# Batch 0 loaded in order of need, last products of batch 0 on VectorE and ACT, projections of quad 1 ahead of the sums of quad 0, scaled values as separate steps

## The chip, the cores and the metric

The kernel runs on one core of a Trainium2 chip. The metric is the device time in microseconds of one execution, the median of several runs. The kernel uses five engines, each with its own instruction queue that is worked through in order: TensorE (PE) for matrix products and transposes, VectorE (DVE), ScalarE (ACT) for exponentials and copies, GpSimd (POOL) for arithmetic on SBUF and for issuing transfers that change the type, and SyncE (SP), which issues transfers. Sixteen transfer engines serve the queues of GpSimd and SyncE. Matrix products land in PSUM; everything else lies in SBUF.

## The reference

Eight batches of eight heads, 576 positions, head size 64, 128 features. Linear attention with exponential features, then one layer of an expert with an ELU:

```
proj = x @ w_phi                                  # x is q or k, per head: 576x64 @ 64x128
phi(x) = [exp(proj - m), exp(-(proj - m))]        # m = max |proj| of the row
kv  = phi(k)^T @ v ;  z = sum over positions of phi(k)
att = (phi(q) @ kv) / (phi(q) . z + 1e-6)
x   = att, heads side by side: 4608 x 512
h   = x @ w_in                                    # 512 x 2048
g   = h if h > 0 else exp(min(h, 0)) - 1
out = g @ w_out                                   # 2048 x 512, fp32
```

## The kernel before

The eight heads of a batch are worked in two quads of four heads; there are 16 quads. Quad i is batch i // 2. Of the 576 positions of a head 512 are the main rows, four to a partition, and 64 are the tail rows, which two heads share in one tile.

A quad has these steps, each a list of small functions in the dictionary that `attention_steps` returns. `tr`: eight transposes and one for the tails on TensorE for k, then for q, each followed by copies out of PSUM (L134, L137). `k`: five projections (four heads and the tails, L153), each with a maximum of |proj| on VectorE (L161) and two exponentials on ACT (EK, L174). The maximum isn't subtracted; instead `scale` takes em = exp(-m) and exp(m) on ACT (L182) and multiplies v by it on GpSimd: a cast (L187), four products of 128x512 (L192) and two of 128x128 (L200); these scaled values are vs. `q`: five projections of q for their maxima alone. `qf`: q's features with positions along the columns (L209, L217), and w = exp(2m). `kv`: the sums phi(k)^T v over positions, two groups of 20 products (L250, L262) with a copy to SBUF by ACT. `out`: four heads and the tails of phi(q) kv (L283, L308), the two signs put together on VectorE (L293, L299), then the division: a reciprocal on VectorE and two products of 128x576 on GpSimd that give x (L331). `x`: nine transposes of x (L341, L353) and two copies into xT.

The expert works on chunks of 512 rows, one for each batch and a ninth for all the tails. A unit of the first product (`mm1`, 16 for a chunk): four matmuls into ph (L386), an exponential on ACT (e_sb, L394), e - 1 on GpSimd (u_sb, L396), and max(ph, min(u, 0)) on VectorE (gT, L399). A unit of the second (`mm2`, four for a chunk): 16 matmuls into po (L407), a copy by ACT, a transfer out. Units are called between the attention's steps when they are due by a steady count of units per slot.

The program goes through slots: slot n does the projections and features of quad n (`new`), the sums of quad n - 1 (`old`), and the transposes of quad n + 1 (`nxt`), in an order that `slot_steps` writes out. Slot 0 has no old quad; slot 2 is the first at whose end the expert has work. The calls are not yet the order of the instructions: a planner orders them for each engine by its own forecast of when each is ready, with the earlier call first among those that are ready, and then sets the semaphores.

Loads: k and q are changed from fp32 to bf16 by the transfer and are issued by GpSimd; v stays fp32 and is issued by SyncE. Batch 0 is loaded in halves (heads 0 to 3 with the tails, then heads 4 to 7). `extra` is a list of further GpSimd transfers (eight of w_in, four calls for k and q of batch 1, eight of w_out), one taken after each step in slots 0 and 1 and after each third step later. `load_v(1)` is called after the scale step of quad 0. Tiles for k, q and v have two buffers, so batch b + 2 is loaded when batch b is done with them; the sums `tot` have one buffer.

## Time and profile before

| | |
|---|---|
| median of 3 runs | 472.37 us (471.5 to 473.35) |
| profiled execution | 472.63 us, span 470.9 us |
| TensorE busy | 406.8 us (86%) |
| VectorE busy | 279.0 us (59%) |
| ACT busy | 262.6 us (56%) |
| GpSimd busy | 247.7 us (53%) |
| chain that ended last | TensorE 51%, GpSimd 20%, ACT 11%, VectorE 8%, issue 5%, transfers 4% |

The span is the time from the first to the last instruction of the profiled execution; its own time has 1.7 us around it. Matmuls are pipelined and their ends are modelled, so a busy TensorE need not run at its peak.

### The profile page before, as it was taken

Reading aid. Unit: us, or ns where it says so; the run is one execution under the profiler, and the core shown is the slowest. Engines: PE = TensorE matmul, PEld = TensorE weight load, DVE = VectorE, ACT = ScalarE, POOL = GpSimd, SP = SyncE. Lnnn points to the kernel's source line nnn. Section 1 sums busy time; section 2 is a strip of 40 time slices with the busy share of each in tenths; the row PEclk is TensorE's granted clock in tenths of the full one; section 3 lists DMA queues with packets and bytes.
Section 4 is the critical chain, followed back from the end, with each engine's and each line's share of the span. In section 5 each row is a group of like instructions: output and inputs, shape, how many; then the busy total and the mean of one; then the engine's idle time right before and its main releaser. Section 6 shows DMA issues by size and latency. Waiting matters only on the chain.

```text
span 470.9 us, 8519 instructions
## 1 busy us (share of the span) xinstructions
PE 406.8 (86%) x3248; PEld 224.3 (48%) x3248; DVE 279.0 (59%) x596; ACT 262.6 (56%) x581; POOL 247.7 (53%) x360
## 2 busy tenths in 40 slices
PE   1674687899989998999898979799869898999995
PEld 0352444455546454646463636365536454444442
DVE  1564465974598359937992577738766755434420
ACT  1563074772888287746764548456738572543431
POOL 6388636836673568445943473716372643423420
PEclk9977787999999999999998999999989999999999
DMA  9999905331723181219201931010000000110113
GB/s 176 230 138 200 223 1 61 42 120 51 107 28 98 58 121 34 74 67 125 94 9 45 141 79 30 1 68 24 2 0 24 22 24 24 45 46 23 46 45 67
DMA packets 46329, 33.12 MB, mean 70 GB/s; under 512 B 14416, under 2 KB 41168, under 8 KB 46288
## 3 DMA queue, kind: packets, MB, share of 16 engines
q0 software_dynamic: 28192, 13.64, 22.6%
q1 hardware_dynamic: 18096, 18.94, 12.8%
q8 instruction: 25, 0.41, 0.4%
q14 instruction: 16, 0.13, 0.1%
HBM read 36.77 MB, written 9.44 MB: 98 GB/s over the span
## 4 chain that ended last, share of the span: by engine, by line
PE 51%; POOL 20%; ACT 11%; DVE 8%; issue 5%; DMA 4%; POOLq 0%; ACTq 0%
PE po L407 23%; PE ph L386 13%; POOL vs L192 7%; ACT EK L174 5%; POOL u_sb L396 4%; DMA q_b<-in_q_dram 4%; POOL x L331 3%; PE pkv L250 3%; DVE gT L399 3%; PE pk L153 3%; ACT e_sb L394 3%; ACT Eq L217 2%; PE tr L133 2%; POOL vs L200 2%; PE tr L341 2%
## 5 line engine op out<-in xcount | busy, mean ns | idle before, releaser
L396 POOL TENSOR_SCALAR u_sb<-e_sb 128x512 bf16<-128x512 f32 x144 | 87.3, 617 | 129.9 <-ACT e_sb L394 120.9
L386 PE MATMUL ph<-xT,w_in_sb 128*128 128x512 bf16 x512 | 139.9, 386 | 12.0 <-DVE gT L399 11.6
L407 PE MATMUL po<-w_out_sb,gT 128*128 128x512 bf16 x576 | 139.7, 383 | 4.2 <-DVE gT L399 4.2
L399 DVE SCALAR_TENSOR_TENSOR gT<-u_sb,ph 128x512 bf16<-128x512 bf16 x144 | 96.6, 681 | 68.5 <-POOL u_sb L396 67.7
L394 ACT ACTIVATE e_sb<-ph 128x512 f32<-128x512 f32 x144 | 86.0, 633 | 47.5 <-PE ph L386 47.3
L407 PEld LDWEIGHTS <-gT 128*128 128x128 bf16 x576 | 54.7, 99 | 63.1 <-DVE gT L399 5.1
L174 ACT ACTIVATE EK<-pk 128x512 bf16<-128x512 f32 x128 | 67.9, 624 | 26.7 <-DVE m_k L161 26.3
L386 PEld LDWEIGHTS <-w_in_sb 128*128 128x128 bf16 x576 | 52.2, 98 | 58.5 <-issue 20.3
L217 ACT ACTIVATE Eq<-pq 128x512 bf16<-128x512 f32 x128 | 65.9, 638 | 18.4 <-PE pq L209 18.3
L192 POOL TENSOR_TENSOR vs<-v_b,em 128x512 bf16<-128x512 f32 x64 | 65.3, 1043 | 17.5 <-ACT em L182 17.4
L415 ACT COPY o_sb<-po 128x512 f32<-128x512 f32 x36 | 21.5, 596 | 82.4 <-PE po L407 76.3
L161 DVE TENSOR_REDUCE m_k<-pk 128x4 f32<-128x512 f32 (+1 forms) x80 | 49.0, 632 | 19.3 <-PE pk L153 19.0
L161 DVE TENSOR_REDUCE m_q<-pk 128x4 f32<-128x512 f32 (+1 forms) x80 | 49.0, 624 | 9.0 <-PE pk L153 8.7
L331 POOL TENSOR_TENSOR x<-tot,rec 128x576 bf16<-128x576 f32 x32 | 36.0, 1146 | 15.7 <-DVE rec L328 15.6
L283 PEld LDWEIGHTS <-Eq 128*128 128x128 bf16 x512 | 29.2, 99 | 22.7 <-issue 9.1
L283 PE MATMUL pn<-kv,Eq 128*128 128x65 bf16 x512 | 33.5, 195 | 2.9 <-ACT EK L174 1.9
L293 DVE TENSOR_TENSOR tot<-pn,w 128x260 f32<-128x260 f32 x64 | 27.0, 422 | 10.4 <-PE pn L283 10.2
L134 DVE COPY kT<-tr 128x1024 bf16<-128x1024 bf16 x16 | 11.0, 690 | 36.6 <-PE tr L133 36.6
L153 PE MATMUL pk<-w_phi_both,qT 128*128 128x256 bf16 x144 | 28.3, 290 | 3.0 <-ACT EK L174 1.8
L153 PE MATMUL pk<-w_phi_both,kT 128*128 128x256 bf16 x144 | 28.9, 295 | 1.8 <-ACT EK L174 0.9
L209 PE MATMUL pq<-qT,w_phi_both 128*128 128x512 bf16 x64 | 22.8, 421 | 4.9 <-DVE m_q L161 2.8
L299 DVE TENSOR_TENSOR tot<-tot,pn 128x260 f32<-128x260 f32 x64 | 26.6, 417 | 0.4
(56 smaller groups left out, 363.5 us busy)
## 6 DMA issues: line engine op xcount, KB each, us to landing
out_dram<-o_sb SPq DMA_DIRECT2D x32, 256.0 KB, 2.3
v_b<-in_v_dram SPq DMA_DIRECT2D x7, 1024.0 KB, 5.7
k_b<-in_k_dram POOLq DMA_DIRECT2D x7, 512.0 KB, 7.8
q_b<-in_q_dram POOLq DMA_DIRECT2D x7, 512.0 KB, 8.2
w_in_sb<-in_moe_w_in_dram POOLq DMA_DIRECT2D x8, 256.0 KB, 12.4
w_out_sb<-in_moe_w_out_dram POOLq DMA_DIRECT2D x8, 256.0 KB, 8.5
v_b<-in_v_dram SPq DMA_DIRECT2D x2, 512.0 KB, 7.2
v_b<-in_v_dram SPq DMA_DIRECT2D x16, 64.0 KB, 5.4
```

Of the source, the lines that this page charges most:

```text
L153: nc.tensor.matmul(pk[:, 2 * j:2 * j + 2, :].rearrange("p a b -> p (a b)"), xT[:, 2 * hh + j, :], w_phi_rhs, start=True, stop=True,)
L161: nc.vector.tensor_reduce(m[:, o:o + NT] if hh < 4 else m[:, NS - 1::NS], pk[:, 0:2 * n, :], axis=AX.X, op=ALU.max, apply_absolute_value=True,
L174: nc.scalar.activation(dst, pk, ACT.Exp, scale=1.0 - 2.0 * sg)
L192: nc.gpsimd.tensor_tensor(vs[:, sg, r, 0:D], vb[:, o:o + 2 * HW].rearrange("p (n d) -> p n d", d=D), em[:, sg, r, None].to_broadcast((P, 2 ...
L217: nc.scalar.activation(st["Eq"][:, par, c, sg, :], pq, ACT.Exp, scale=1.0 - 2.0 * sg)
L283: nc.tensor.matmul(pt[:, t, :], st["Eq"][:, par, c, sg, o:o + P], st["kv"][:, s, c, sg, :], start=True, stop=True,)
L331: nc.gpsimd.tensor_tensor(st["x"][:, :, c, :], st["tot"][:, r, 0:D], rec[:, r, None].to_broadcast((P, NS, D)), op=ALU.mult,)
L386: nc.tensor.matmul(ph, w_in_sb[:, ct, jt * P:(jt + 1) * P], xTs[ch][:, ct, :], start=(ct == 0), stop=(ct == N_CT - 1),)
L394: nc.scalar.activation(e_sb, ph, ACT.Exp)
L396: nc.gpsimd.tensor_scalar(u_sb, e_sb, -1.0, 1.0, op0=ALU.add, op1=ALU.mult)
L399: nc.vector.scalar_tensor_tensor(gTs[ch][:, jt, :], u_sb, 0.0, ph, op0=ALU.min, op1=ALU.max)
L407: nc.tensor.matmul(po, gT[:, jt, tt * P:(tt + 1) * P], w_out_sb[:, jt, :], start=(jt == 0), stop=(jt == N_JT - 1),)
```

## The change

- Transfers of batch 0: v's first half with its tails and v's second half are issued by GpSimd, behind k and q of the same half, instead of by SyncE. Three of the w_in transfers are called before slot 0; the rest of `extra` is taken after steps 17 and later of slot 0, after each step of slot 1 and each third step later.
- `load_v(1)` is called after the scale step of quad 1. Instead of a memset, VectorE copies a column of em of quad 1 into the first column of v's main and tail parts, so that the load depends on em.
- The copies of q's transposes are on ACT instead of VectorE for both quads of batch 0.
- The scaled values and the two products of the division are on VectorE instead of GpSimd for quad 1.
- `k_scale` keeps em and the cast; the six products become steps `vs` of their own, `v_scaled`, with new places in each slot.
- Slot 0: the transposes of quad 1 come after the second q projection. Slot 1: the k projections and em of quad 1 come first, then kv of quad 0, then q projections of quad 1, sums of quad 0 and vs of quad 1 in turn. x_out of quad 0 moves from the end of slot 1 to behind kv of quad 1 in slot 2.

The whole diff, without its unchanged surroundings where they say nothing:

```diff
@@ -118,9 +118,11 @@
             )
 
 
+    states = {}
+
     def attention_steps(i):
         b, qd = divmod(i, 2)
-        st = {}
+        st = states[i] = {}
 
         def transposes(n):
             src = kqv[b][n]
@@ -131,10 +133,11 @@
             for j in range(8):
                 o = m0 + j * P
                 nc.tensor.transpose(tr[:, j, :], src[:, o:o + P], ident)
-            nc.vector.tensor_copy(dst[:, 0:8, :], tr)
+            copy = nc.scalar.copy if n == 1 and b == 0 else nc.vector.tensor_copy
+            copy(dst[:, 0:8, :], tr)
             trt = apsum.tile([P, P], BF16, name="trt", tag="ap")
             nc.tensor.transpose(trt, src[:, t0:t0 + P], ident)
-            nc.vector.tensor_copy(dst[:, 8, :], trt)
+            copy(dst[:, 8, :], trt)
             if n == 0:
                 st["m_k"] = small.tile([P, 2 * NS], FP32, name="m_k")
                 st["EK"] = work.tile([P, 4, 2, NT * F], BF16, name="EK")
@@ -176,33 +179,32 @@
         def q_head(hh):
             project(st["qT"], hh, st["m_q"])
 
+
+        eng = nc.vector if i == 1 else nc.gpsimd
+
         def k_scale():
-            em = small.tile([P, 2, 2 * NS], FP32, name="em")
+            em = st["em"] = small.tile([P, 2, 2 * NS], FP32, name="em")
             for sg in range(2):
                 nc.scalar.activation(
                     em[:, sg, :], st["m_k"], ACT.Exp, scale=2.0 * sg - 1.0
                 )
-            vb = kqv[b][2]
             vs = st["vs"] = work.tile([P, 2, 2 * NS, D1], BF16, name="vs")
-            nc.gpsimd.tensor_copy(vs[:, :, :, D], em)
-            for c in range(2):
-                for sg in range(2):
-                    r = slice(c * NS, c * NS + 2 * NT)
-                    o = (4 * qd + 2 * c) * HW
-                    nc.gpsimd.tensor_tensor(
-                        vs[:, sg, r, 0:D],
-                        vb[:, o:o + 2 * HW].rearrange("p (n d) -> p n d", d=D),
-                        em[:, sg, r, None].to_broadcast((P, 2 * NT, D)),
-                        op=ALU.mult,
-                    )
-            t0 = BW + qd * P
-            for sg in range(2):
-                nc.gpsimd.tensor_tensor(
-                    vs[:, sg, NS - 1::NS, 0:D],
-                    vb[:, t0:t0 + P].rearrange("p (n d) -> p n d", d=D),
-                    em[:, sg, NS - 1::NS, None].to_broadcast((P, 2, D)),
-                    op=ALU.mult,
-                )
+            eng.tensor_copy(vs[:, :, :, D], em)
+
+        def v_scaled(sg, c):
+
+            if c < 2:
+                r = slice(c * NS, c * NS + 2 * NT)
+                o, n = (4 * qd + 2 * c) * HW, 2 * NT
+            else:
+                r = slice(NS - 1, None, NS)
+                o, n = BW + qd * P, 2
+            eng.tensor_tensor(
+                st["vs"][:, sg, r, 0:D],
+                kqv[b][2][:, o:o + n * D].rearrange("p (n d) -> p n d", d=D),
+                st["em"][:, sg, r, None].to_broadcast((P, n, D)),
+                op=ALU.mult,
+            )
 
         def q_features(par, c):
             pq = apsum.tile([P, 4 * P], FP32, name="pq", tag="ap")
@@ -328,7 +330,7 @@
             nc.vector.reciprocal(rec, den)
             for c in range(2):
                 r = slice(c * NS, (c + 1) * NS)
-                nc.gpsimd.tensor_tensor(
+                eng.tensor_tensor(
                     st["x"][:, :, c, :],
                     st["tot"][:, r, 0:D],
                     rec[:, r, None].to_broadcast((P, NS, D)),
@@ -366,6 +368,7 @@
             "tr": [each(transposes, n) for n in range(2)],
             "k": [each(k_head, hh) for hh in range(5)],
             "scale": [k_scale],
+            "vs": [each(v_scaled, sg, c) for c in range(3) for sg in range(2)],
             "q": [each(q_head, hh) for hh in range(5)],
             "qf": [each(q_features, par, c) for c in range(2) for par in range(2)]
             + [q_features_tail],
@@ -451,24 +454,38 @@
 
     def slot_steps(n):
         old, new, nxt = quads.get(n - 1), quads.get(n), quads.get(n + 1)
-        if not old:
-            return new["k"] + new["scale"] + new["q"] + new["qf"] + nxt["tr"]
+        if n == 0:
+            return (
+                new["k"] + new["scale"] + new["q"][:2] + nxt["tr"] + new["q"][2:]
+                + new["vs"] + new["qf"]
+            )
+        if n == 1:
+            steps = new["k"] + new["scale"] + old["kv"]
+            for j in range(5):
+                steps += new["q"][j:j + 1] + old["out"][j:j + 1]
+                steps += new["vs"][j:j + 1]
+            return steps + new["vs"][5:] + new["qf"] + nxt["tr"]
         if n == 2:
 
             return (
-                old["kv"] + old["out"] + old["x"]
+                old["kv"] + quads[0]["x"] + old["out"] + old["x"]
                 + [lambda: chunk_ready(0)]
-                + new["k"] + new["scale"] + new["q"] + new["qf"] + nxt["tr"]
-            )
-        none = {"k": [], "q": [], "scale": [], "qf": []}
-        kk, qq = (new or none)["k"], (new or none)["q"]
+                + new["k"] + new["scale"] + new["q"] + new["vs"] + new["qf"]
+                + nxt["tr"]
+            )
+        none = {"k": [], "q": [], "scale": [], "qf": [], "vs": []}
+        new = new or none
+        kk, qq, vv = new["k"], new["q"], new["vs"]
         steps = (
             old["kv"][:1] + kk[:1] + old["kv"][1:] + kk[1:3]
             + old["out"][:1] + kk[3:4] + old["out"][1:2] + kk[4:]
-            + (new or none)["scale"]
-            + old["out"][2:3] + qq[:1] + old["out"][3:4] + qq[1:2]
-            + old["out"][4:] + qq[2:] + (new or none)["qf"]
-        )
+            + new["scale"]
+            + old["out"][2:3] + vv[:1] + qq[:1] + old["out"][3:4] + vv[1:2]
+            + qq[1:2] + old["out"][4:] + vv[2:3]
+            + qq[2:4] + vv[3:4] + qq[4:]
+        )
+        for j in range(5):
+            steps += new["qf"][j:j + 1] + vv[4 + j:5 + j]
         if nxt:
             steps += nxt["tr"]
         steps += old["x"]
@@ -482,18 +499,15 @@
     wst = consts.tile([P, F], FP32)
     for c in range(2):
         nc.sync.dma_start(out=wst[c * D:(c + 1) * D, :], in_=w_phi)
-    for n in range(2):
+    for n in range(3):
         load_main(nc.gpsimd, n, 0, 0, 4)
         load_tails(nc.gpsimd, n, 0)
-    load_main(nc.sync, 2, 0, 0, 4)
-    load_tails(nc.sync, 2, 0)
     nc.vector.memset(w_phi_both, 0.0)
     for c in range(2):
         r = slice(c * D, (c + 1) * D)
         nc.vector.tensor_copy(w_phi_both[r, c, :], wst[r, :])
-    for n in range(2):
+    for n in range(3):
         load_main(nc.gpsimd, n, 0, 4, 8)
-    load_main(nc.sync, 2, 0, 4, 8)
 
     quads[0] = attention_steps(0)
     for step in quads[0]["tr"]:
@@ -509,17 +523,21 @@
             )
         ]
 
-    def load_v(b, gate=False):
-        if gate:
-            nc.vector.memset(kqv[b][2][:, 0:1], 0.0)
+    def load_v(b, after=None):
+        if after is not None:
+
+            for o in (0, BW):
+                nc.vector.tensor_copy(kqv[b][2][:, o:o + 1], after)
         load_main(nc.sync, 2, b, 0, 8)
         load_tails(nc.sync, 2, b)
 
-    extra = [
+    w_in_loads = [
         lambda ct=ct, c=c: load_w_in(ct, c) for ct in range(N_CT) for c in range(2)
     ]
-    extra += load_kq(1)
-    extra += [lambda jt=jt: load_w_out(jt) for jt in range(0, N_JT, 2)]
+    w_out_loads = [lambda jt=jt: load_w_out(jt) for jt in range(0, N_JT, 2)]
+    for f in w_in_loads[:3]:
+        f()
+    extra = w_in_loads[3:] + load_kq(1) + w_out_loads
 
     UNITS = 136
     done = 0
@@ -533,9 +551,9 @@
         steps = slot_steps(n)
         for j, step in enumerate(steps):
             step()
-            if n == 0 and step is quads[0]["scale"][0]:
-                load_v(1, gate=True)
-            if extra and (n < 2 or j % 3 == 2):
+            if n == 1 and step is quads[1]["scale"][0]:
+                load_v(1, after=states[1]["em"][:, 0, 0:1])
+            if extra and ((n == 0 and j > 16) or n == 1 or j % 3 == 2):
                 extra.pop(0)()
             due = (n + (j + 1) / len(steps) - 2.5) * UNITS / 14.5
             while done < due and (first or second):
```

## Rows read from the trace of the kernel before

**Rows 1.** Busy time by stretches: us, engine busy (instructions), granted clock, DMA share, GB/s written.

```profile
0.00:60.00 60.00, 31.21 (x288) 20.60 (x289) 25.87 (x62) 21.79 (x51) 39.10 (x60) 0.85 1.11 190
60.00:100.00 40.00, 32.95 (x278) 19.23 (x276) 29.74 (x61) 28.11 (x66) 25.82 (x38) 0.88 0.37 60
100.00:400.00 300.00, 276.60 (x2382) 154.74 (x2381) 201.50 (x442) 186.60 (x421) 163.11 (x230) 0.98 0.25 54
```

**Rows 2.** Timeline of TensorE, prologue: start, us, instructions [idle before <-releaser].

```profile
14.55 0.26 PE L136 MATMUL trt<-ident,q_b 128*128 128x128 bf16 x1 [1.25 <-DMA q_b<-in_q_dram]
...
48.30 1.03 PE L341 MATMUL tr<-ident,x 128*128 128x128 bf16 x8 [6.24 <-POOL x L331]
...
51.91 0.56 PE L283 MATMUL pn<-kv,Eq 128*128 128x65 bf16 x8
...
59.10 1.03 PE L341 MATMUL tr<-ident,x 128*128 128x128 bf16 x8 [3.46 <-POOL x L331]
...
60.03 1.91 PE L153 MATMUL pk<-w_phi_both,kT 128*128 128x256 bf16 x8
```

**Rows 3.** Timeline of all engines and queues, first 10 us.

```profile
0.95 0.06 DVE L514 MEMSET v_b<- 128x1 f32 x1
...
4.00 1.24 SPq L103 DMA_DIRECT2D v_b<-in_v_dram  x2
```

**Rows 4.** Timeline of GpSimd, prologue.

```profile
12.50 0.52 POOL L78 DMA_DIRECT2D w_in_sb<-in_moe_w_in_dram  x1 [3.23 <-DMA q_b<-in_q_dram]
...
25.73 1.61 POOL L78 DMA_DIRECT2D w_in_sb<-in_moe_w_in_dram  x3
...
39.00 2.13 POOL L83 DMA_DIRECT2D w_out_sb<-in_moe_w_out_dram  x3 [1.28 <-DMA q_b<-in_q_dram]
...
41.27 4.06 POOL L192 TENSOR_TENSOR vs<-v_b,em 128x512 bf16<-128x512 f32 x4
...
46.00 2.25 POOL L331 TENSOR_TENSOR x<-tot,rec 128x576 bf16<-128x576 f32 x2
```

**Rows 5.** Timeline of ACT: em of quad 1.

```profile
33.55 0.34 ACT L182 ACTIVATE em<-m_k 128x18 f32<-128x18 f32 x2
```

**Rows 6.** Waits of TensorE, 60 us to the end: us in total, times, longest.

```profile
PE ph L386 <- DVE gT L399: 11.6, 9, 3.5
PE po L407 <- DVE gT L399: 4.2, 2, 2.3
```

**Rows 7.** Timeline of GpSimd around one of these waits.

```profile
273.52 1.04 POOL L192 TENSOR_TENSOR vs<-v_b,em 128x512 bf16<-128x512 f32 x1 [0.92 <-ACT em L182]
...
278.42 2.35 POOL L396 TENSOR_SCALAR u_sb<-e_sb 128x512 bf16<-128x512 f32 x4
```

**Rows 8.** Timeline of TensorE: the same wait, and the first kv product after it.

```profile
279.80 0.59 PE L386 MATMUL ph<-xT,w_in_sb 128*128 128x512 bf16 x2 [3.26 <-DVE gT L399]
...
288.18 0.67 PE L250 MATMUL pkv<-vs,EK 128*128 128x65 bf16 x16
```

**Rows 9.** Busy time of the stretch behind that wait, columns as in rows 1.

```profile
279.80:283.50 3.70, 3.70 (x12) 1.39 (x12) 3.70 (x11) 1.68 (x3) 2.47 (x4) 0.66 0.98 299
```

**Rows 10.** Busy time with both transfer queues, then GpSimd's alone; columns as in rows 1.

```profile
4.00:23.00 19.00, 8.81 (x42) 4.86 (x43) 7.56 (x14) 6.43 (x16) 8.11 (x13) 1.00 1.23 237
28.00:38.00 10.00, 7.50 (x72) 4.65 (x70) 8.71 (x20) 5.36 (x14) 7.18 (x11) 0.67 1.33 185
```

**Rows 11.** Line 113 (tail loads), first 110 us: from issue to landing.

```profile
DMA to landing us min/median/max: 2.7/6.7/16.4
```

**Rows 12.** Groups by shape: count, busy us, mean ns of one, idle before.

```profile
L399 DVE SCALAR_TENSOR_TENSOR gT<-u_sb,ph 128x512 bf16<-128x512 bf16 x144 | 96.6, 681 | 68.5 <-POOL u_sb L396 67.7
...
L192 POOL TENSOR_TENSOR vs<-v_b,em 128x512 bf16<-128x512 f32 x64 | 65.3, 1043 | 17.5 <-ACT em L182 17.4
...
L299 DVE TENSOR_TENSOR tot<-tot,pn 128x260 f32<-128x260 f32 x64 | 26.6, 417 | 0.4
...
L415 ACT COPY o_sb<-po 128x512 f32<-128x512 f32 x36 | 21.5, 596 | 82.4 <-PE po L407 76.3 <-issue 4.4 <-ACT Eqt L232 0.9
```

## The prediction

> **What bounds the kernel now.** I read the busy time by stretches first [rows 1]. TensorE is busy 276.6 of the 300 us from 100 to 400 but only 31.2 of the first 60. So there are two places to gain: 28.8 us idle in the prologue, and some 23 us of holes in the middle.
>
> The prologue next, by timelines. TensorE still waits for the tail rows of q of quad 0 at 14.55, and the projections of k, which need nothing of q, stand behind them in its queue [rows 2]. Why q is late: it shares the transfer engines with v. SyncE sends the rest of v of batch 0 and all of v of batch 1 from 4.00 on [rows 3]. The memset of L514, which should hold back the load of batch 1, ran at 0.95: it depends on nothing, and the planner put it first, although the program calls it after the scale step [rows 3]. So program order is only a wish here; a data dependence binds.
>
> Then GpSimd [rows 4]. Its twelfth transfer (w_in, 12.50) waits for the landing of its fourth (q's main rows), its 28th (w_out, 39.00) for its 20th (q's main rows of batch 1). So eight are in flight at most, and the next blocks the engine, arithmetic included. The scaled values of quad 1 could start when em is there, at 33.89 [rows 5]; they start at 41.27 behind the w_out issues, x of quad 0 follows at 46.00 to 48.25, and TensorE waits 6.24 us for that x at 48.30 [rows 2, 4]. For x of quad 1 it waits 3.46 us more at 59.10. The projections of quad 2 begin at 60.03; from there both kernels have the same work left.
>
> In the middle I read the waits: after 60 TensorE waited 11.6 us (ph) and 4.2 us (po) for gT [rows 6]. One case: GpSimd does the cast and all six vs pieces from 273.52 to 278.42 without a break, four u_sb stand behind them, and TensorE is idle 3.26 us until 279.80 [rows 7, 8]. The granted clock of the 3.7 us that follow is 0.66, so a part of them ran at 1.2 GHz and the rest at 2.4, after that idle time [rows 9].
>
> **The change part by part.** Times are of the profiled execution: 472.63 us beside a span of 470.9, 0.26 above the median of 472.37.
>
> *Loads in order of need.* The four transfers that bring v of quad 0 and the main rows of quad 1 move to GpSimd's queue behind k and q, and v of batch 1 waits for em of quad 1. Issuing costs some 0.54 each, as at 25.73 [rows 4], while GpSimd had only blocked issues to do. Up to q's tails its queue has to bring 256 + 64 + 256 + 64 KB = 0.655 MB. Alone it moved 185 GB/s, both queues together 237 [rows 10], so alone it takes 3.5 us, after a first issue at about 2 and a landing time of at least 2.7 us for tails [rows 11], which are issued by about 5.8. So q is complete at about 9; bounds 8.5, and 14.5 if nothing is won. I take 9: 5.5 us earlier, and all of slot 0 with it. vs(0), over at 25.73, is then over at about 20.4.
>
> *q copies of batch 0 on ACT.* ACT takes 596 ns for 512 columns [rows 12], so at most 1.2 us for 1024 and less for the tail. The first pair lies in ACT's idle start; the second is put into its row of exponentials: 0 to 1.5 us, and I take 0 for the end, because em(1) has slack against the transfers below.
>
> *Quad 1's projections ahead of quad 0's sums.* em(1) no longer waits for kv(0). I count only slot 0's 5.5 us: 33.89 becomes 28.4; bounds 26 and 30.
>
> *Last products of batch 0 on VectorE.* The trace has no such product there. Between 417 ns for 260 columns and 681 for 512 [rows 12] I take 0.68 for 512, 0.77 for 576, 0.42 at most for 128; lower bound 0.42 each. vs(1) costs 4 x 0.68 + 2 x 0.42 = 3.6 us, against the 4.7 from 41.27 to 46.00 on GpSimd [rows 4], and no longer stands behind w_out. With eight sums (8 x 0.417) and five maxima (about 0.68 each) beside it, VectorE needs some 10 us from 28.4: 38.5. x(1) costs 1.5 instead of 2.25 us.
>
> No VectorE form of rows 12 has both inputs in SBUF (pn and ph are PSUM tiles), and GpSimd's 512-column product takes 1043 ns on average there. The Trainium skill ("SBUF — State Buffer", Who interferes with whom) says that a VectorE instruction with two SBUF inputs contends with GpSimd instructions that read SBUF, and that the loser blocks fully. vs(1) and x(1) are such instructions. By that rule they would cost up to 3.6 + 1.5 us on one of the two engines, and the sum below would be 5.1 us longer; no row shows it.
>
> *What is late next.* q of batch 1. In the old kernel GpSimd resumed issuing at 25.73 and those rows landed at 39.00 [rows 4]. Now it resumes at 20.4, with five w_in instead of three left: 1.31 + 1.18 MB at 185 GB/s from about 22 end at 35.5; but v of batch 1 (1.18 MB) now falls into this stretch, and 3.67 MB at 237 end at 37.5. I take 38.5 for uneven queues. The last w_out issues wait for it as before, so GpSimd is free at about 41 and x(0) ready at 43.3. kv(1) stands behind quad 2's transposes, which need the same q; it takes 51.91 - 48.30 - 0.93 = 2.7 us (0.93 is x_out, 59.10 to 60.03) [rows 2], now ahead of x_out(0) and hidden by x(0). From x(0) to quad 2's projections the old kernel needed 11.7 us (48.30 to 60.03); less 2.7 and less 0.75 for x(1) that is 8.3: 51.6 instead of 60.03. I take **9 us** won, with a little for fewer issues in front. Bounds: 14, if q of batch 1 is there at 34; 4, if GpSimd is free only at 45.
>
> *vs as separate steps.* Nothing is added; products of 1.04 us [rows 12] now alternate with the units' u_sb. What can be won is 15.8 us of waiting [rows 6] and the low clock behind the long waits, (1 - 0.66) x 3.7 = 1.3 us in the one shown [rows 9], some four times: 5. GpSimd has about 8 us of work in the 10 around each (4.9 vs, the rest u_sb [rows 7]), so some waiting stays. Bounds 0 and 20.8; I take half, **10.5 us**.
>
> *Extra DMA issues at other steps*: the same transfers, a slot ahead of their need. I take 0; bounds -1 and +1.
>
> Sum: 472.6 - 9 - 10.5 = 453.1.
>
> **The rivals.**
> 1. *The transfers keep the prologue.* GpSimd stays blocked until q of batch 1 lands, at 39 in the old kernel and with v beside it perhaps at 43, and x(0) falls where it was. For it: the two issue waits of rows 4, and a planner that moves a memset ahead of everything. Against: q of batch 0, vs(1) and x(1) leave that queue in any case. Only the middle gains: 462.1. Chance 0.13.
> 2. *The middle keeps its waits.* The planner goes by its own forecast of what is ready, and may leave GpSimd's pieces together. Against: in the case of rows 7 the u_sb stand right behind the last piece, so they are called in the same stretch. Only the prologue gains: 463.6. Chance 0.20.
> 3. *Slower: scaled values come too late.* vs ended at 278.42 and its reader, kv, ran at 288.18 [rows 7, 8]: 9.8 us to spare. The last piece now comes after the second feature step, 5 of 33 steps before the end of a slot of 22.8 us (60.03 to 288.18 is ten slots): 3.5 us to spare. Four u_sb (2.35) [rows 7], an x (2.25) [rows 4] and the piece itself (1.04 at most) make 5.6, so kv stalls up to 2.1 us in each of 13 slots, 27 us: 472.6 - 9 + 27 = 490.6. It decides from 1.5 us a slot, where it eats both gains. Against: u_sb seldom queue four deep once vs is split. Chance 0.05.
> 4. *The two-SBUF products and GpSimd block each other* in batch 0, for their 5.1 us: 458.2. For it speaks only the skill's sentence above; against it no row. Chance 0.05.
> 5. *The change does not do what it says*: the planner puts the steps back into the old order, and 472 stays. Only v's dependence and the engines are fixed by data. Chance 0.03.
>
> **How the numbers follow.** The likeliest (both gains) has 0.54, and the prediction is its 453.1, given as 453. The range of 441 to 465 takes in rivals 1, 2 and 4, and leaves out 3 and 5 and the ends of the likeliest. Faster by over 0.5% (about what a measurement of this kernel can tell from no change): 0.54 + 0.13 + 0.20 + 0.05 = 0.92; within 0.5%: 0.03; slower: 0.05.
>
> **What would show it.** Right: q's transposes at 8 to 9.5; vs(0) over near 20; vs(1) on VectorE over before 40; v of batch 1 issued after 25; quad 2's projections at 48 to 54; u_sb between vs pieces, and waits for gT after 60 under 8 us in all, with a higher clock from 60 to 100. Wrong in the prologue: x(0) on GpSimd still past 46, behind w_out. Wrong in the middle: vs pieces in one block, or TensorE waiting at each slot's first pkv. If quad 2 starts early and the end does not move as much, the time went to the middle.

## The result, and the profile after

The changed kernel takes 448.28 us (447.22 to 448.56), the kernel before 472.81 (471.5 to 473.35) beside it: ratio 0.9481, 95% interval 0.9455 to 0.9507. So 24.5 us went, where the forecast had 19.5. The changed kernel run again on another occasion gave 448.16 (445.65 to 448.9), ratio 0.9495 (0.9457 to 0.9533). The execution profiled here took 447.22 us with a span of 445.4.

Busy time by stretches, columns as in [rows 1]:

```profile
0.00:60.00 60.00, 37.13 (x316) 23.90 (x319) 35.27 (x80) 30.98 (x73) 37.21 (x59) 0.83 1.13 190
60.00:100.00 40.00, 35.55 (x329) 20.73 (x334) 29.83 (x62) 27.16 (x65) 28.53 (x42) 1.00 0.41 73
100.00:400.00 300.00, 283.05 (x2368) 158.51 (x2411) 206.31 (x442) 192.07 (x426) 167.56 (x238) 1.00 0.26 56
```

TensorE is 5.9 us busier in the first 60, and from 60 on the granted clock is 1.00 (2.4 GHz throughout), where [rows 1] show 0.88 and 0.98. In the trace of the second occasion it is 0.96 from 60 to 100 and 1.00 from 100 to 400. Transfers move the same 190 GB/s.

TensorE in the prologue (start, us, instructions, idle before and its releaser), beside [rows 2]:

```profile
8.80 1.03 PE L135 MATMUL tr<-ident,q_b 128*128 128x128 bf16 x8 [1.10 <-DMA q_b<-in_q_dram]
...
40.66 1.01 PE L135 MATMUL tr<-ident,q_b 128*128 128x128 bf16 x8 [0.55 <-DVE kT L137]
...
41.57 1.00 PE L252 MATMUL pkv<-vs,EK 128*128 128x65 bf16 x16
...
43.57 0.62 PE L343 MATMUL tr<-ident,x 128*128 128x128 bf16 x8
...
50.67 0.62 PE L343 MATMUL tr<-ident,x 128*128 128x128 bf16 x8 [2.59 <-DVE x L333]
...
51.18 0.60 PE L156 MATMUL pk<-w_phi_both,kT 128*128 128x256 bf16 x4
```

q of quad 0 is transposed at 8.80 instead of 14.55. x of quad 0 (43.57) is waited for no longer, where it had cost 6.24 us, and quad 2's projections begin at 51.18 instead of 60.03. GpSimd in the same stretch, beside [rows 4]:

```profile
17.74 2.09 POOL L202 TENSOR_TENSOR vs<-v_b,em 128x512 bf16<-128x512 f32 x2
19.73 0.57 POOL L78 DMA_DIRECT2D w_in_sb<-in_moe_w_in_dram  x1
20.32 2.41 POOL L202 TENSOR_TENSOR vs<-v_b,em 128x512 bf16<-128x512 f32 x3
22.67 0.96 POOL L103 DMA_DIRECT2D k_b<-in_k_dram  x1
...
33.27 2.12 POOL L83 DMA_DIRECT2D w_out_sb<-in_moe_w_out_dram  x3 [1.21 <-DMA q_b<-in_q_dram]
37.81 2.25 POOL L333 TENSOR_TENSOR x<-tot,rec 128x576 bf16<-128x576 f32 x2 [2.43 <-DVE rec L330]
```

Its vs pieces of quad 0 now have transfer issues between them. It waits for q of batch 1 only until 33.27 (39.00 before) and is free at 35.4. Then it waits for VectorE (the reciprocal), not for a transfer. VectorE:

```profile
28.77 2.90 DVE L202 TENSOR_TENSOR vs<-v_b,em 128x512 bf16<-128x512 f32 x6
31.58 0.42 DVE L295 TENSOR_TENSOR tot<-pn,w 128x260 f32<-128x260 f32 x1
...
37.45 0.27 DVE L330 RECIPROCAL rec<-den 128x18 f32<-128x18 f32 x1
...
49.19 1.43 DVE L333 TENSOR_TENSOR x<-tot,rec 128x576 bf16<-128x576 f32 x2
```

It works from 27.83 to 37.7 without a gap: vs of quad 1, then the maxima of q in turn with the sums. ScalarE, beside [rows 5]:

```profile
27.37 0.54 ACT L188 ACTIVATE em<-m_k 128x18 f32<-128x18 f32 x2
...
36.75 4.03 ACT L219 ACTIVATE Eq<-pq 128x512 bf16<-128x512 f32 x8 [6.82 <-PE pq L211]
```

Behind the prologue, the waits of TensorE for gT from 60 us on (us, times, longest), beside [rows 6], where they were 15.8 us in 11 waits:

```profile
PE ph L389 <- DVE gT L402: 6.9, 11, 2.2
```

GpSimd in a slot of the middle, beside [rows 7]:

```profile
168.73 1.05 POOL L202 TENSOR_TENSOR vs<-v_b,em 128x512 bf16<-128x512 f32 x1
...
171.91 0.61 POOL L399 TENSOR_SCALAR u_sb<-e_sb 128x512 bf16<-128x512 f32 x1
172.50 1.40 POOL L202 TENSOR_TENSOR vs<-v_b,em 128x512 bf16<-128x512 f32 x2
173.87 0.61 POOL L399 TENSOR_SCALAR u_sb<-e_sb 128x512 bf16<-128x512 f32 x1
174.45 0.39 POOL L202 TENSOR_TENSOR vs<-v_b,em 128x128 bf16<-128x128 f32 x1
```

u_sb stands between vs pieces, where four had stood behind all six. The reader of these pieces, on TensorE, beside the last of [rows 8]:

```profile
178.53 0.67 PE L252 MATMUL pkv<-vs,EK 128*128 128x65 bf16 x16
```

It starts 3.7 us after the last piece is over (174.84) and waits for nothing.

**Where the 24.5 us went.** In the two profiles 8.85 us lie before quad 2's projections (60.03 to 51.18). From there to the end the kernel before needs 470.9 - 60.03 = 410.9 us and the changed one 445.4 - 51.18 = 394.2: 16.65 us. Together that is 25.5, the difference of these two executions; the medians differ by 24.5. The second half is the larger.

### The profile page after: what moved, and what is told of

The parts are those of the page before. It is cut to its first block, busy times and chain, and to the rows that moved or that the text cites. A ratio compares the mean times of both kernels' runs of the same rounds, so it can differ in the third digit from the quotient of the medians.

```text
span 445.4 us, 8463 instructions
## 1 busy us (share of the span) xinstructions
PE 396.4 (89%) x3194; PEld 221.5 (50%) x3248; DVE 283.8 (64%) x602; ACT 264.6 (59%) x585; POOL 243.8 (55%) x355
## 3 DMA queue, kind: packets, MB, share of 16 engines
q0 software_dynamic: 28544, 14.82, 24.8%
## 4 chain that ended last, share of the span: by engine, by line
PE 54%; ACT 14%; DVE 13%; POOL 11%; issue 5%; DMA 1%; POOLq 0%; ACTq 0%
PE po L410 24%; PE ph L389 13%; ACT EK L177 5%; ACT Eq L219 5%; POOL u_sb L399 4%; POOL vs L202 4%; PE pk L156 4%; DVE gT L402 4%; PE pkv L252 3%; PE tr L135 3%; ACT e_sb L397 2%; POOL x L333 2%; DVE m_q L164 2%; DVE m_k L164 2%; PE pn L285 2%
## 5 line engine op out<-in xcount | busy, mean ns | idle before, releaser
L389 PE MATMUL ph<-xT,w_in_sb 128*128 128x512 bf16 x480 | 130.5, 379 | 8.8 <-DVE gT L402 6.9
L410 PE MATMUL po<-w_out_sb,gT 128*128 128x512 bf16 x556 | 134.5, 379 | 0.8
L202 POOL TENSOR_TENSOR vs<-v_b,em 128x512 bf16<-128x512 f32 (+1 forms) x90 | 73.0, 830 | 27.4 <-ACT em L188 27.3
L285 PEld LDWEIGHTS <-Eq 128*128 128x128 bf16 x512 | 30.2, 99 | 26.3 <-issue 10.5
L333 POOL TENSOR_TENSOR x<-tot,rec 128x576 bf16<-128x576 f32 x30 | 33.8, 1145 | 10.0 <-DVE rec L330 9.8
L285 PE MATMUL pn<-kv,Eq 128*128 128x65 bf16 x512 | 34.6, 196 | 4.9 <-DVE tot L295 1.1
L252 PE MATMUL pkv<-vs,EK 128*128 128x65 bf16 x512 | 22.9, 198 | 1.9 <-ACT EK L177 1.2
```

Source lines behind the costliest of these rows:

```text
L202: eng.tensor_tensor(st["vs"][:, sg, r, 0:D], kqv[b][2][:, o:o + n * D].rearrange("p (n d) -> p n d", d=D), st["em"][:, sg, r, None].to_bro ...
L285: nc.tensor.matmul(pt[:, t, :], st["Eq"][:, par, c, sg, o:o + P], st["kv"][:, s, c, sg, :], start=True, stop=True,)
L333: eng.tensor_tensor(st["x"][:, :, c, :], st["tot"][:, r, 0:D], rec[:, r, None].to_broadcast((P, NS, D)), op=ALU.mult,)
L389: nc.tensor.matmul(ph, w_in_sb[:, ct, jt * P:(jt + 1) * P], xTs[ch][:, ct, :], start=(ct == 0), stop=(ct == N_CT - 1),)
L410: nc.tensor.matmul(po, gT[:, jt, tt * P:(tt + 1) * P], w_out_sb[:, jt, :], start=(jt == 0), stop=(jt == N_JT - 1),)
```

## The experiments

Each was run beside the kernel before on the same chip; ratios are to that, with their 95% interval. Kernels without an interval in the text are compared by the times in their profiles.

**1. The split alone.** The kernel before, with vs as steps from quad 3 on in the places that the changed kernel gives them.

```diff
...
-            "scale": [k_scale],
+            "scale": [scale_all] if i < 3 else [k_scale],
+            "vs": [] if i < 3 else vs_steps,
...
-            + old["out"][2:3] + qq[:1] + old["out"][3:4] + qq[1:2]
-            + old["out"][4:] + qq[2:] + (new or none)["qf"]
+            + old["out"][2:3] + vv[:1] + qq[:1] + old["out"][3:4] + vv[1:2]
+            + qq[1:2] + old["out"][4:] + vv[2:3]
+            + qq[2:4] + vv[3:4] + qq[4:]
...
+        for j in range(5):
+            steps += new["qf"][j:j + 1] + vv[4 + j:5 + j]
```

> The kernel before with one part of the change: from quad 3 on the six products of v are steps of their own, in the places that the change gives them; the prologue is as before. Theory (the block of products on GpSimd starves the units): 16 us less than before, about 456.5, and waits of TensorE for gT after quad 2 fall from some 12 us to under 5. Rival (the time after the prologue fell because the units start earlier against the slots, not because of the split): 470 or more, with waits for gT as before.

Measured: 458.5 us (457.57 to 460.02), ratio 0.9763 (0.9721 to 0.9804), by which it is about 11 us. Its waits for gT from 60 us on, and its stretch 100 to 400:

```profile
PE ph L390 <- DVE gT L403: 7.4, 11, 3.2
```

```profile
100.00:400.00 300.00, 286.24 (x2433) 158.94 (x2432) 206.23 (x448) 191.08 (x428) 168.37 (x238) 1.00 0.26 56
```

The waits are halved and the clock of that stretch goes from 0.98 to 1.00 with nothing else changed. The split does both.

**2. The split undone.** The changed kernel, with vs in one block again from quad 3 on.

```diff
...
-            "scale": [k_scale],
-            "vs": [each(v_scaled, sg, c) for c in range(3) for sg in range(2)],
+            "scale": [k_scale] if i < 3 else [scale_all],
+            "vs": [each(v_scaled, sg, c) for c in range(3) for sg in range(2)] if i < 3 else [],
```

> The changed kernel with the six products of v in one block behind em again from quad 3 on; the prologue stays changed. Theory: the long waits for gT come back, 448 + 15 = about 463, and quad 2's projections still begin at 51. Rival (the start of the units against the slots did it): 449 or less.

Measured: 460.09 us (459.84 to 461.6), ratio 0.9792 (0.9757 to 0.9828). Quad 2's projections begin at 51.55, within 0.4 us of the changed kernel; from there its profile needs 458.1 - 51.55 = 406.6 us instead of 394.2. The waits are those of [rows 6] again:

```profile
PE ph L395 <- DVE gT L408: 10.3, 8, 3.5
PE po L416 <- DVE gT L408: 4.2, 2, 2.3
```

So the split is worth 12.3 us by the profiles here, and the rest of the change 10 by the ratio. The two parts add up to most of it: 11 from the first run and 10 from this are 21 of 24.5, and each has an interval of some 2 us to either side.

**3. The loads' order alone.** The kernel before, with all transfers of batch 0 on GpSimd's queue in order of need, v of batch 1 behind em of quad 1, and the w_in transfers moved as in the change (three ahead of slot 0, the rest of `extra` from step 11 of slot 0).

```diff
...
-    for n in range(2):
+    for n in range(3):
         load_main(nc.gpsimd, n, 0, 0, 4)
         load_tails(nc.gpsimd, n, 0)
-    load_main(nc.sync, 2, 0, 0, 4)
-    load_tails(nc.sync, 2, 0)
...
-            if n == 0 and step is quads[0]["scale"][0]:
-                load_v(1, gate=True)
+            if n == 1 and step is quads[1]["scale"][0]:
+                load_v(1, after=ems[1][:, 0, 0:1])
```

> The kernel before with the loads alone changed: v of batch 0 on GpSimd's queue behind k and q, v of batch 1 after em of quad 1, three w_in ahead and the rest from step 11 of slot 0. Theory (GpSimd's queue, with quad 1's products behind the transfer issues, is what holds the prologue): q is there at 9 and slot 0 ends 5 us earlier, but vs of quad 1 still waits behind w_out, so quad 2's projections begin at 56 to 59 and the whole gains 2 to 4 us, about 470. Rival (order of loads is the whole of the prologue's gain): projections at 51, 464.

Measured: 471.45 us (469.93 to 472.83), ratio 1.001 (0.9983 to 1.0037): nothing, against 2 to 4 us expected. q is transposed at 8.77, but quad 2's projections begin at 61.44. GpSimd shows why:

```profile
16.31 4.04 POOL L194 TENSOR_TENSOR vs<-v_b,em 128x512 bf16<-128x512 f32 x4
20.32 0.76 POOL L202 TENSOR_TENSOR vs<-v_b,em 128x128 bf16<-128x128 f32 x2
21.03 2.14 POOL L78 DMA_DIRECT2D w_in_sb<-in_moe_w_in_dram  x4
...
40.35 2.12 POOL L83 DMA_DIRECT2D w_out_sb<-in_moe_w_out_dram  x3 [4.12 <-DMA q_b<-in_q_dram]
...
47.35 2.25 POOL L333 TENSOR_TENSOR x<-tot,rec 128x576 bf16<-128x576 f32 x2
```

Now that SyncE's queue is empty in this stretch, everything comes by GpSimd's, and GpSimd issues nothing from 16.31 to 21.03. The transfers that it had in flight run out. The stretch 20 to 24 of this kernel, then of the changed one, then 24 to 28 of the kernel before:

```profile
20.00:24.00 4.00, 3.62 (x59) 2.78 (x59) 2.37 (x7) 2.90 (x9) 4.00 (x8) 1.00 0.42 74
```

```profile
20.00:24.00 4.00, 1.95 (x8) 0.89 (x8) 2.12 (x4) 4.00 (x12) 3.97 (x7) 0.73 1.07 213
```

```profile
24.00:28.00 4.00, 3.43 (x44) 2.93 (x42) 1.94 (x5) 2.39 (x7) 4.00 (x8) 0.62 0.35 54
```

74 GB/s instead of 213. The kernel before has such a hole too (54 GB/s, behind its products from 21.02 to 25.78), but by 24 us SyncE's queue had moved v of both batches there (2.43 MB, with w_phi). Here v of batch 1 is issued at 28.28, and all of its 1.18 MB comes by SyncE's queue before q of batch 1, which GpSimd issued at 25.27, behind the hole. That q is there at 40.35, later than in the kernel before (39.00), and all that slot 0 had won is given back.

**4. The loads' order, and quad 0's vs as steps.** As experiment 3, with one transfer issued after each of quad 0's vs steps.

```diff
...
-            return new["k"] + new["scale"] + new["q"] + new["qf"] + nxt["tr"]
+            return (
+                new["k"] + new["scale"] + new["q"] + new["vs"] + new["qf"]
+                + nxt["tr"]
+            )
```

> The run with the loads alone, and besides the six products of quad 0 as steps of their own after its q projections, with a transfer issue called after each. Theory (in the run with the loads alone the block of products on GpSimd from 16.3 to 21.0 kept further loads from being issued; the transfer engines stood at a share of 0.42 from 20 to 24 and q of batch 1 landed at 40): the issues now run between the products, q of batch 1 lands at 34 to 36, quad 2's projections begin 4 us earlier than in that run, 467. Rival (v of batch 1 beside it is what makes q late): 471 as there.

Measured: 467.61 us (464.18 to 468.54), ratio 0.9898 (0.9847 to 0.9949): 4.8 us, as expected. 20 to 24 moves 210 GB/s, and:

```profile
17.20 1.08 POOL L202 TENSOR_TENSOR vs<-v_b,em 128x512 bf16<-128x512 f32 x1
18.19 0.57 POOL L78 DMA_DIRECT2D w_in_sb<-in_moe_w_in_dram  x1
...
33.13 2.14 POOL L83 DMA_DIRECT2D w_out_sb<-in_moe_w_out_dram  x3 [1.00 <-DMA q_b<-in_q_dram]
```

q of batch 1 comes 7.2 us earlier than in experiment 3, and quad 2's projections at 55.22, 6.2 us earlier. Two things differ. The hole is filled: (210 - 74) GB/s x 4 us is 0.5 MB, by estimate 2.6 us at 210. And v of batch 1 comes behind q instead of ahead of it: em of quad 1, on which its load depends, is over at 31.05 instead of 28.14, so the load is issued at 31.94, and up to q's landing SyncE's queue moved 0.07 MB, against 1.25 in experiment 3; by the same estimate that is 5.6 us. So the expectation's rival seems to hold for the larger part, and no run tells what filling the hole would win by itself.

**5. Quad 1's products back on GpSimd.** The changed kernel but for one line.

```diff
-        eng = nc.vector if i == 1 else nc.gpsimd
+        eng = nc.gpsimd
```

> The changed kernel with quad 1's scaled values and division on GpSimd again; all else stays. Theory: vs of quad 1 stands behind the w_out issues, which end at 35.4, so it runs 35.5 to 40.5, x of quad 0 after it or before it, and x of quad 1 takes 2.25 instead of 1.43 us: quad 2's projections begin 2 to 4 us later, about 451. Rival (VectorE's row is what holds the prologue now, since quad 1's maxima and quad 0's sums stand behind vs on it): 447 to 448, no loss, because VectorE loses 3.3 us of work.

Measured: 450.83 us (449.83 to 452.11), ratio 0.959 (0.9553 to 0.9627). vs of quad 1 stands behind the w_out issues again (37.20 to 41.2, the last two pieces behind x of quad 0 at 43.43), x of quad 1 takes 2.25 us instead of 1.43, and quad 2's projections begin at 53.78, 2.6 us later. With the 4.8 us of experiment 4 that is 7.4 of the 8.85 us before quad 2's projections.

**6. The old order of slots 0 to 2.** The changed kernel, with quad 0's sums ahead of quad 1's projections again.

```diff
...
-        if n == 1:
-            steps = new["k"] + new["scale"] + old["kv"]
-            for j in range(5):
-                steps += new["q"][j:j + 1] + old["out"][j:j + 1]
-                steps += new["vs"][j:j + 1]
-            return steps + new["vs"][5:] + new["qf"] + nxt["tr"]
...
-                old["kv"] + quads[0]["x"] + old["out"] + old["x"]
+                old["kv"] + old["out"] + old["x"]
```

> The changed kernel with the order of slots 0 to 2 as before: transposes of quad 1 at the end of slot 0, kv and sums of quad 0 ahead of quad 1's k projections, x of quad 0 at the end of slot 1. Loads, engines and separate vs steps stay as changed. Theory (order, engines and loads each give a few us, and the order gives em of quad 1 and with it vs on VectorE earlier): quad 2's projections 2 to 4 us later than 51, about 451. Rival (order is what makes the loads count, since alone they gave nothing): projections at 57 or later, 455.

Measured: 447.46 us (447.01 to 449.74), ratio 0.9494 (0.9452 to 0.9535). Quad 2's projections begin at 51.03. VectorE's row holds the same work in another order and ends at 37.5 instead of 37.7. This part of the change is worth nothing that can be told here, and both expectations missed.

**7. v of batch 1 early.** The changed kernel, with that load issued at quad 0's scale step and no dependence.

```diff
-            if n == 1 and step is quads[1]["scale"][0]:
-                load_v(1, after=states[1]["em"][:, 0, 0:1])
+            if n == 0 and step is quads[0]["scale"][0]:
+                load_v(1)
```

> The changed kernel, but v of batch 1 (1.15 MB) is issued by SyncE at quad 0's scale step, without waiting for em of quad 1. Theory (the wait for em holds 1.15 MB back from the transfers of k and q of batch 1, which GpSimd's queue sits behind): at 213 GB/s it takes 5.4 us from them, q of batch 1 lands at 38.7 instead of 33.3, GpSimd is free of w_out's issues at about 40.8 instead of 35.4, x(0) ends at about 45.5, its use by the transposes of x near 46 to 47, and quad 2's projections begin at 53 to 54 instead of 51.2: 450 to 451. Rival (the second queue brings its bytes beside the first, or the prologue's chain through ScalarE and VectorE has slack for all of it): q of batch 1 lands before 35, quad 2's projections begin within 0.5 us of 51.2, and the time is 447.5 to 449.

Measured: 450.29 us (449.87 to 451.77), ratio 0.9565 (0.9507 to 0.9624), the theory's size, but not its place. TensorE at the start:

```profile
9.84 0.27 PE L139 MATMUL trt<-ident,k_b 128*128 128x128 bf16 x1 [3.09 <-DMA k_b<-in_k_dram]
...
11.57 1.03 PE L135 MATMUL tr<-ident,q_b 128*128 128x128 bf16 x8 [1.46 <-DMA q_b<-in_q_dram]
```

Without the dependence v of batch 1 is issued at 2.00, ahead of what slot 0 needs, and slot 0 is late: q of quad 0 is transposed at 11.57 instead of 8.80. These 2.77 us go through nearly unchanged: em of quad 1 2.8 us later, vs of quad 1 at 31.42 instead of 28.77, the reciprocal at 40.09 instead of 37.45, quad 2's projections at 53.87 instead of 51.18. So this run tells what v's dependence is worth (2.7 us), and nothing of whether q of batch 1 has slack.

**8 to 10. More steps ahead.** Three ways to use ScalarE's idle time in the changed kernel: 8.80 us before 52.85 (the first and second) and 6.82 us before 36.75 (the second and third). First, k and em of quad 2 ahead of kv and the sums of quad 1; `mixed` is the sums of quad 1, the q projections and vs of quad 2 in turn:

```diff
...
-                old["kv"] + quads[0]["x"] + old["out"] + old["x"]
-                + [lambda: chunk_ready(0)]
-                + new["k"] + new["scale"] + new["q"] + new["vs"] + new["qf"]
-                + nxt["tr"]
+                new["k"] + new["scale"] + old["kv"] + quads[0]["x"] + mixed
+                + old["x"] + [lambda: chunk_ready(0)]
+                + new["qf"] + nxt["tr"]
```

> The changed kernel with slot 2 ordered like slot 1: k projections and em of quad 2 first, then kv of quad 1, x of quad 0, sums of quad 1 and q projections and vs of quad 2 in turn. Theory: ACT stood idle for 8.8 us from 44 to 52.9 in the changed kernel, waiting for quad 2's maxima; this work moves into the gap, vs of quad 2 is over on GpSimd before the units begin, so the wait for gT of 2.2 us at 61 goes, and the whole gains 3 to 5 us, about 444. Rival (x of quad 1 sets the start of the units, and VectorE's row up to it grows by quad 2's maxima): 449 to 451.

Measured: 447.49 us (447.07 to 448.66), ratio 0.949 (0.9447 to 0.9533). The waits for gT fall to 4.4 us, but x of quad 0 and of quad 1 are transposed at 47.77 and 58.48 instead of 43.57 and 50.67, and the first chunk's matmuls begin at 50.85 instead of 45.43; that this eats the gain is likely and was not tried. Second, that kernel with the first q features of quad 1 ahead of quad 0's sums as well:

```diff
-            steps = new["k"] + new["scale"] + old["kv"]
+            steps = new["k"] + new["scale"] + old["kv"] + new["qf"][:4]
...
```

> As the run with quad 2's k projections ahead, and besides the four feature steps of quad 1 ahead of the sums of quad 0 in slot 1. Theory: ACT stood idle 6.8 us from 29.9 to 36.8 in the changed kernel though features need no maxima; they now run there, the transposes of quad 2 and kv of quad 1 stand 3 to 5 us earlier behind them, and the whole gains 2 to 3 us more than the run without, about 442. Rival (VectorE, busy without a break from 27.8 to 37.7, sets when kv of quad 1 and x of quad 0 are ready): no more than 0.5 us against the run without.

Measured: 445.86 us (445.24 to 446.61), ratio 0.9451 (0.9415 to 0.9487), 1.6 us below its neighbour. Third, that line in the changed kernel itself, beside the changed kernel again; `mixed` is here q and vs of quad 2 in turn, then its features with the last vs behind the first of them:

```diff
...
-                + new["k"] + new["scale"] + new["q"] + new["vs"] + new["qf"]
-                + nxt["tr"]
+                + new["k"] + new["scale"] + mixed + nxt["tr"]
```

> The changed kernel once more, as the yardstick for the variant beside it on the same chip. Every theory expects 447 to 449 and a ratio within 0.946 to 0.951 of the kernel before.

> The changed kernel with two edits: the four first feature steps of q of quad 1 stand ahead of quad 0's sums (as in the variant that gained 1.6 us over its neighbour), and in slot 2 quad 2's vs steps stand between its q and feature steps instead of in a row after q; the k steps of quad 2 stay where the changed kernel has them. Theory (the prologue's chain runs through ScalarE and VectorE, and the first features fill the 6.8 us in which ScalarE stood idle before 36.75): x of quad 1 ends some 1.5 us earlier than at 50.6 and quad 2's projections begin near 49.7 instead of 51.2; the wait for the first gT (2.2 us at 61.2) falls below 1.5: 2 to 3 us under the changed kernel run beside it. Rival (quad 0's sums come later by what the features take, and x of quad 1 with them): within 0.7 us of the changed kernel run beside it.

Measured: 448.14 us (447.39 to 449.89), ratio 0.9513 (0.9481 to 0.9544), beside 448.16 and 0.9495 for the changed kernel: the rival. x of quad 1 is transposed at 50.81, no earlier than 50.67. So no version beats the changed kernel by more than can be told: the best, the second, has an interval that overlaps with that of the changed kernel.

**11. Two products of each quad on VectorE.** The changed kernel, from quad 3 on.

```diff
-            eng.tensor_tensor(
+            on = nc.vector if i > 2 and c == 0 else eng
+            on.tensor_tensor(
```

> The changed kernel, but from quad 3 on two of the six products of vs of each quad (the first two of 128x512) are VectorE's: 24 products in 12 quads. Theory (GpSimd no longer sets the time behind the prologue, so relief of it is worth nothing): GpSimd loses 24 x 1.04 = 25 us of work, VectorE gains 24 x 0.69 = 16.5 us, each of which stands ahead of a gT; the waits of TensorE for gT stay within 5 to 15 us in sum (6.9 in the changed kernel's trace behind 60 us) and the time within 447 to 451. Rival A (a VectorE product with both inputs in SBUF and GpSimd's reads lock each other out): the means of u_sb (615 ns), vs (1043 ns) and x (1146 ns) on GpSimd, or of the product on VectorE (686 ns beside GpSimd's DMA issues in the prologue), rise by several per cent, with single ones longer by up to 0.7 us; at 24 x 0.7 = 17 us in all and about a third of it on the path, 453 to 455. Rival B (the first wait left, gT behind vs, is still GpSimd's fault): waits for gT under 4 us and a time of 445 to 446.

Measured: 453.46 us (451.51 to 454.79), ratio 0.9619 (0.9562 to 0.9676), some 5 to 6 us above the changed kernel, the size of rival A. (From quad 3 on there are 13 quads, so 26 products moved, not 24.) GpSimd's timeline, then VectorE's:

```profile
77.11 1.04 POOL L203 TENSOR_TENSOR vs<-v_b,em 128x512 bf16<-128x512 f32 x1
...
96.78 1.57 POOL L203 TENSOR_TENSOR vs<-v_b,em 128x512 bf16<-128x512 f32 x1 [7.20 <-ACT em L188]
```

```profile
77.21 1.50 DVE L203 TENSOR_TENSOR vs<-v_b,em 128x512 bf16<-128x512 f32 x1
...
96.77 0.68 DVE L203 TENSOR_TENSOR vs<-v_b,em 128x512 bf16<-128x512 f32 x1
```

Each pair overlaps. The one that starts first takes its usual time (1.04, 0.68), and the other is longer by most of what is left of it: 0.68 becomes 1.50, with 0.94 left, and 1.04 becomes 1.57, with 0.67 left. By shape over 60 to 400 us (count, busy us, mean ns of one, idle before), on GpSimd and on VectorE:

```profile
L400 POOL TENSOR_SCALAR u_sb<-e_sb 128x512 bf16<-128x512 f32 x123 | 77.7, 641 | 102.2 <-ACT e_sb L398 93.0 <-DVE tot L296 3.9 <-DVE tot L319 1.8
L203 POOL TENSOR_TENSOR vs<-v_b,em 128x512 bf16<-128x512 f32 x29 | 34.7, 1199 | 16.6 <-ACT em L188 16.6
```

```profile
L203 DVE TENSOR_TENSOR vs<-v_b,em 128x512 bf16<-128x512 f32 x26 | 23.1, 887 | 1.4 <-ACT em L188 1.3
```

In the changed kernel's trace these means are 615, 1043 and (in the prologue) 686 ns, so the two lose 123 x 0.026 + 29 x 0.156 + 26 x 0.201 = 13 us to each other in these three groups. The Trainium skill ("SBUF — State Buffer", Who interferes with whom) says that a VectorE instruction with two SBUF inputs and a GpSimd instruction that reads SBUF contend, that the port pair which they share is an exclusive lock, and that the order of issue decides which of them blocks; these pairs agree with it.

What the 5 to 6 us come from is only in part clear. TensorE's waits for gT are about the same (6.8 us). New behind quad 2's projections are 5.0 us in 13 waits for VectorE's sums and maxima (pk for tot 2.4, pnt and pk for m_q 1.7 and 0.9). So VectorE's row is what grew, and it grew by the 26 products themselves (26 x 0.686 = 18 us) as well as by the 5.2 us for which they were blocked. No run separates the two: products that don't meet GpSimd's could have cost time here too.

## Why the prediction was right, point by point

- *Loads in order of need*: right on q (8.80, said 9), on v of batch 1 (issued at 28.95, said after 25) and on em of quad 1 (over at 27.9, said 28.4). Quad 0's vs is over at 24.06, not 20.4, since issues stand between its pieces; that is a gain, not a cost (experiments 3 and 4), and the working did not see it. By its steps the early loads alone should have won some of the 9 us; alone they win nothing, for the hole and for v of batch 1 ahead of q (experiment 3).
- *q copies on ACT*: em(1) is on time with them. They were not tried by themselves.
- *Quad 1's projections ahead of quad 0's sums*: the forecast counted only slot 0's 5.5 us here and nothing for the order. Right: the old order costs nothing (experiment 6).
- *Last products on VectorE*: vs of quad 1 took 2.9 us (forecast 3.6) and x 1.43 (forecast 1.5). The means (686 and 755 ns) are close to the 0.68 and 0.77 taken from [rows 12]; the 128-column ones took 289 ns, under the 0.42 at most. The whole step is worth 2.6 us (experiment 5).
- *What is late next*: **this step failed, though its sum (51.6) is within 0.4 us of 51.18.** It put q of batch 1 at 38.5, GpSimd free at 41, x(0) at 43.3 and everything after behind them. Measured: 33.27, 35.4 and 40.06, and TensorE does not wait for x(0) at all. The sum has 1.18 MB of v of batch 1 beside them; in fact SyncE's queue had moved 0.09 MB in all when q landed. And GpSimd issued again from 16.20, between the vs pieces, not from 20.4; its queue alone moved 225 GB/s from 8 to 20 us, 213 from 20 to 24 and 176 from 24 to 28.9, where [rows 10] gave 185. In its place the chain runs through ScalarE's exponentials (to 27.9) and VectorE's unbroken row (27.83 to 37.7), then q's features on ScalarE (36.75 to 41.4), the transposes of quad 2 and kv of quad 1 at 41.57. Two errors offset each other, so that the sum comes out is luck: the transfers were put 5 us too late, and the way from there to quad 2's projections, 51.6 - 38.5 = 13.1 us in the forecast, took 51.18 - 33.27 = 17.9, because it begins not at the landing but behind VectorE's row, whose end had been forecast well (38.5). That this row sets the prologue is read from the waits (2.43 us for the reciprocal on GpSimd, 6.82 on ScalarE), from the chain that ended last, which runs through the row from 27.83 to 35.35, and from experiment 7, where 2.7 us at its head came out whole at its end. No run shortened the row alone.
- *vs as separate steps*: right in mechanism. Forecast 10.5; measured about 11 us alone and 12.3 by the profiles on top of the prologue. Behind quad 2's projections the profiles differ by 16.65, and the forecast took the work there as the same but for the split. Its time is not quite: four kernels with vs in one block need 410.9 (before), 407.8 (experiment 3), 410.5 (experiment 4) and 406.6 us (experiment 2) from there on, so up to 4.3 of the 16.65 us come and go without the split, and why they do stays open. The two terms can be read apart in experiment 1, which changes nothing else. The kernel before and experiment 1, each from quad 2's projections to the end:

```profile
60.03:470.90 410.87, 375.56 (x2962) 203.69 (x2960) 253.14 (x534) 240.84 (x530) 208.65 (x300) 0.97 0.25 53
```

```profile
59.09:455.80 396.71, 371.94 (x2963) 201.71 (x2960) 254.13 (x534) 240.94 (x530) 209.06 (x300) 0.99 0.26 55
```

  The same matmuls keep TensorE busy for 3.6 us less, at a granted clock of 0.99 instead of 0.97, and it is idle for 10.5 us less (35.3 to 24.8), of which the waits for gT are 8.4 (15.8 to 7.4). The forecast had 2.5 and 7.9, so both terms are too small. For the clock the working took only the few us behind four long waits [rows 9], while [rows 1] have 0.88 over the 40 us from 60 to 100. For the whole change the trace of experiment 7 can stand, which needs the same 394.2 us behind quad 2's projections (the changed kernel's own trace lacks some 50 matmul records): 6.8 us less busy and 9.9 less idle.
- *The rivals*: 1 (transfers keep the prologue) is what experiment 3 shows, with v of batch 1 ahead of q and the split in quad 0 left out; here it did not occur. 2: waits halved, not kept. 3 (slower): the last piece leaves 3.7 us to its reader, said 3.5, and its price did not come up, since u_sb does not queue four deep in the slot shown. 4: vs(1) stands beside transfer issues alone, and GpSimd is idle at x(1), so no arithmetic met there; where it meets, they do block each other (experiment 11). 5: v's dependence, the engines and the split all show in the rows.

## What to carry to other kernels

When an engine both issues transfers and computes, a block of arithmetic on it is a hole in the transfers: put issues between its pieces before you move all loads to its queue, and see which other load gets ahead of the one that is waited for meanwhile. Splitting a block that others queue behind can give back more than the waits in the list: in experiment 1 10.5 us of idle time, with 8.4 in the list, and 3.6 us of busy time at a higher clock. A step moved to an engine with idle time can still lose: it lengthens that engine's row by its own time, and by more where its operands meet the first engine's (experiment 11).

## What the runs showed of the hardware

- VectorE products with two SBUF inputs and GpSimd's reads of SBUF exclude each other for most of the overlap, in both directions (experiment 11: 0.68 to 1.50 us, 1.04 to 1.57), but GpSimd's transfer issues at 29.94 to 32.06 beside vs of quad 1 left VectorE's mean at 686 ns.
- With GpSimd's queue alone and 4.7 us of products without an issue (16.31 to 21.03), the transfer rate was 74 GB/s from 20 to 24 us; with issues between the products it was 210 and 213 (experiments 3 and 4, the changed kernel).
- The 237 and 185 GB/s of [rows 10] are no matter of one or two queues: alone, GpSimd's queue moved 225 GB/s from 8 to 20 us in the changed kernel and 176 from 24 to 28.9.
- The clock of the prologue differs between executions of one kernel: over 40 to 60 us it was 0.94 in the trace shown and 0.79 in that of the second occasion, where quad 2's projections begin at 52.41 instead of 51.18 and the span is 446.7 instead of 445.4.
